# Weight splits shared out by turns, and zero products beside the weight statistics, in an attention-and-MLP kernel

## The chip, the core and the metric

The kernel runs on one core of a Trainium2 chip. The metric is device time in microseconds (us), the median of the runs. TensorE (PE in the profile, with its weight loads as PEld) multiplies, VectorE (DVE), ScalarE (ACT) and GpSimd (POOL) work element by element, and SyncE (SP) and ScalarE issue the DMAs. Each engine works through its own queue in order.

## What is computed

Causal attention with a linear memory read beside it, and a gated MLP behind it:

```python
scores = scale * q @ k.T                       # B, H, S, D = 4, 8, 576, 64, causal
local = softmax(scores) @ v
q_p = where(q > 0, q, exp(q) - 1) + 1
mem_out = (q_p @ M_prev) / (q_p @ z_prev + 1e-6)
attn = g * mem_out + (1 - g) * local           # g = sigmoid(beta), per head
x = attn.reshape(2304, 512)
xn = x / sqrt(mean(x * x) + 1e-6) * rms_g
h = silu(xn @ w_gate) * (xn @ w_val)           # 512 -> 1536
out = h @ w_out                                # 1536 -> 512
```

The weights arrive as 64-bit floats. Products are made exact enough by splitting each operand into a 16-bit high part and a 16-bit low part and adding three products (high with high, high with low, low with high).

## The kernel before, in words

The 2304 tokens are 18 blocks of 128 rows; two blocks form a chunk of 256, so there are nine chunks. Attention runs block by block in units of one to four heads: scores (line 443, PE), scaling and mask (L449, DVE), exponential (L495, ACT), high part (L497, ACT), low part (L506, DVE, or POOL for blocks 2 and 3), transposition (by PE for blocks 0 and 1, by DMA from block 2 on) and the product with v (L530 to L532). A finished block is normed and split into x (`x_split`, L621). A chunk's projections need x of both of its blocks.

**The weights.** `w_gate` and `w_val` are cut into 24 pieces of 128 x 512: three thirds t of the 1536 columns, in each eight pieces p. A piece passes four steps. `load_w` (L659) brings its raw words into a ring of five places; the load of piece p+5 is issued from ACT's queue once piece p is converted. `w_conv` (L975) converts it: ACT L687 and DVE L691 and L692 write one float32 piece into the tile `wgv`. `gram` (L128, products on L135) forms sums of squares on PE, from which `gv_scales` (L702) makes the third's scales `rgs` once its eighth piece is through. `w_split` (L737) then scales the piece and splits it into high and low part. With `SPLIT` at "3" (`split`, L89) this is: DVE scales in place (L99), ACT rounds to the high part (L101), POOL subtracts for the low part (L104). `w_out` passes the same steps in twelve pieces of its own (`wo_conv`, `wo_split`, tile `wo`).

**Places in `wgv`.** The tile has 25 places, and a place holds either one float32 piece or one pair of high and low part. Piece p lies as float32 in place p+1 and its split goes into place p. So a split writes where the piece before it was read from: the high part of piece p+1 (L101) waits until POOL has finished L104 of piece p. At the start, places 17 to 24 hold the early k and v blocks that `first_gram` reads.

**Projections.** For column block F of a chunk, `m_proj` (L750) makes 24 products of 128 x 256 into `gv` (L762), `m_act` (L765) and `m_split` (L778) form the hidden values, and `m_down` (L805, L816 to L818) multiplies them with `w_out`. The names gv0 to gv11 below are chunk 0's column blocks; gv0 to gv3 need the first third of the weights, gv4 to gv7 the second, gv8 to gv11 the last. gv12 begins chunk 1.

**What sets the order.** The program is written as lists of steps that are dealt out beside each other (`zipped`, `run`, L1049 to L1077): conversion and splitting of third 0 beside the first two blocks, of third t beside the projections of the third before it. The framework's scheduler then fixes the order in each engine's queue from priorities and its own idea of durations, so that a change of one step moves others.

Of the kernel before, what the change touches and what calls it, by code (L numbers as in the profile page):

```python
# [9 lines left out]
F32 = mybir.dt.float32  # L10
F16 = mybir.dt.float16
BF16 = mybir.dt.bfloat16
# [19 lines left out]
A3 = 0.2  # L32
A4 = 0.3
C2 = 8
SPLIT = ("3", "3", "3", "3")
VWAY = "11"
RING = 5
PACE = 5
NTP = 2
PRIO = (500, 600, 100)  # L40
NPM = 2
NPOOL = (4, 8)
# [3 lines left out]
def attn_memory_moe_kernel(  # L46
# [81 lines left out]
    def gram(acc, src, first, last):  # L128

        hi = src.bitcast(BF16).rearrange("p (f w) -> p f w", w=2)[:, :, 1]
        for g in range(4):
            w = hi[:, g * P : (g + 1) * P]
            nc.tensor.matmul(acc[:, :P], w, w, start=first and g == 0, stop=last and g == 3)  # L135

    csum = {}

# [97 lines left out]

    def load_pre(n):

        at = 1 + 4 * NC + 2 * (n - NI)
        pre[n] = wgv[:, at : at + 2, :]  # L240
        nc.sync.dma_start(out=pre[n], in_=qkv[n, :, :2, :])

# [390 lines left out]
    def piece(m, cc, t):  # L633
        return t * 2 * NC + m * NC + cc

    raws = {}
    NR = RING

# [63 lines left out]
    def gv_scales(t):  # L702
# [1 line left out]

        c = wt[:, t]
        mx = tiny.tile([P, 2], F32, tag="mx", name="wmx", bufs=2)
        nc.vector.tensor_reduce(mx, csum.pop(t), axis=AX.X, op=ALU.max)
        nc.vector.tensor_scalar(c[:, 6:8], over_partitions(mx, 2), gmax2, 1.03, op0=ALU.mult, op1=ALU.mult)
        pow2_scales(c[:, 6:8], 2, c[:, 0:2], c[:, 2:4])

# [25 lines left out]

    def w_split(m, cc, t):  # L737
        p = piece(m, cc, t)
        src = wgv[:, p + 1, :]
        sc = rgs[:, t, m, cc : cc + 1]  # L740
        split(wgv16[:, p, :512], wgv16[:, p, 512:], src, sc, way_of(SPLIT, t, p % (2 * NC)))

# [232 lines left out]
    def w_conv(i):  # L975
        m, cc, t = pcs[i]
        p = piece(m, cc, t)
        f64_to_f32(raws.pop(p), wgv[:, 1 + p, :], i)
        held.pop(p)
        if cc == m == 0:  # L980
            csum[t] = ps.tile([P, 2, P], F32, tag="out", name="csum")
        gram(csum[t][:, m], wgv[:, 1 + p, :], cc == m == 0, cc == NC - 1 and m == 1)
        if i + PACE < len(pcs):
            load_w(*pcs[i + PACE])

    def wo_conv(f):
        f64_to_f32(raws.pop(("o", f)), wo[:, 1 + f, :], len(pcs) + f)
        held.pop(("o", f), None)
        if f == 0:
            csum["o"] = ps.tile([P, 512], F32, tag="out", name="csum")  # L990
        gram(csum["o"], wo[:, 1 + f, :], f == 0, f == NF - 1)
        for nx in {0: (3,), 1: (4,), 2: (5,), 3: (6,), 4: (7,), 6: (8, 9), 8: (10,), 10: (11,)}.get(f, ()):
            load_wo(nx)

# [144 lines left out]
```

## Time and profile before

| what | us |
|---|---|
| median of three runs (lowest, highest) | 685.72 (685.72, 687.58) |
| the profiled execution's own time | 687.62 |
| its span, first to last instruction | 685.9 |
| PE busy in the span (2592 products of L762 alone) | 597.1 (363.4) |
| DVE, ACT, POOL busy | 480.8, 406.9, 232.3 |
| mean granted TensorE clock, as a share of 2.4 GHz | 0.938 |

A slice of the page is 685.9 / 40 = 17.1 us. Busy digits are tenths of a slice; the PEclk line gives the clock granted to TensorE in tenths of 2.4 GHz, so that 5 stands for 1.2 GHz all through and what lies between for a mixture. Shares over the whole span hide that the first 184 us and the rest have different limits, so the stretches are read apart.

### The profile page before, as it was taken

The page shows a single profiled execution, that of the slowest core. Times are in us where ns is not written, and L with a number is a line of the kernel's source. Part 1 is how long each engine was busy: PE and PEld are TensorE (multiplying, and loading weights), DVE is VectorE, ACT ScalarE, POOL GpSimd, SP SyncE. Part 2 cuts the span into 40 slices and gives each one's busy share as a digit, 9 for nine tenths or more (in the row PEclk, how much of TensorE's full clock was granted, in tenths as well). Part 3 has the DMA queues.
Part 4 walks back from the last instruction along what each step waited for, and adds up shares of the span by engine and source line. Part 5 has one row for each costly group of instructions (what it writes and reads, how often), then busy time and mean ns, then how long its engine had stood idle before and what let it go on. Part 6 is the DMA issues. An engine that isn't in the chain of part 4 may idle for free.

```text
span 685.9 us, 16422 instructions
## 1 busy us (share of the span) xinstructions
PE 597.1 (87%) x6292; PEld 461.3 (67%) x6292; DVE 480.8 (70%) x1441; ACT 406.9 (59%) x845; POOL 232.3 (34%) x308
## 2 busy tenths in 40 slices
PE   2664367866899999999899999999999999999997
PEld 1553245745665587778678777767777878887774
DVE  3689997985685766679687776786887686873221
ACT  5788655665647676657556657766666464442322
POOL 1306544674467434323025231431322222212111
PEclk9985567977899999999999999999999999999999
DMA  8952589833935968844675865376664554441001
GB/s 271 411 148 83 188 272 227 184 77 80 176 69 89 191 126 166 166 88 88 118 155 123 167 131 113 64 137 142 123 131 103 107 78 93 80 76 34 32 1 31
DMA packets 186383, 88.13 MB, mean 128 GB/s; under 512 B 171712, under 2 KB 171712, under 8 KB 186304
## 3 DMA queue, kind: packets, MB, share of 16 engines
q1 hardware_dynamic: 181392, 70.81, 49.5%
q10 hardware_dynamic: 4912, 16.28, 7.1%
q8 instruction: 49, 0.80, 0.5%
q14 instruction: 30, 0.25, 0.1%
HBM read 36.20 MB, written 4.72 MB: 60 GB/s over the span
## 4 chain that ended last, share of the span: by engine, by line
PE 43%; DVE 17%; DMA 16%; ACT 13%; issue 5%; POOL 4%; SPq 1%; ACTq 0%; DVEq 0%; POOLq 0%
PE gv L762 23%; DMA kv<-in_qkv_dram 6%; DMA PT<-P 5%; PE out L816 4%; PE out L817 4%; PE out L818 4%; DVE S L449 3%; ACT junk L220 2%; PE sc L443 2%; DMA qT<-row 2%; ACT P L497 2%; PE sc L469 2%; ACT S L495 2%; DVE P L506 2%; DMA phT<-row 2%
## 5 line engine op out<-in xcount | busy, mean ns | idle before, releaser
L762 PE MATMUL gv<-xT,wgv 128*128 128x256 f16 x2592 | 363.4, 279 | 11.7 <-DVE th L772 6.4
L762 PEld LDWEIGHTS <-wgv 128*128 128x128 f16 x2592 | 253.2, 100 | 56.0 <-issue 7.6
L794 POOL TENSOR_TENSOR h<-th,h 128x256 f16<-128x256 f32 x96 | 71.5, 745 | 259.3 <-ACT h L793 201.2
L495 ACT ACTIVATE S<-S,nm 128x128 f32<-128x128 f32 (+4 forms) x144 | 80.2, 586 | 57.3 <-DVE nm L456 42.2
L443 PE MATMUL sc<-kT,qT 128*128 128x128 f16 x640 | 94.9, 224 | 12.9 <-DMA kT<-row 4.1
L506 DVE TENSOR_TENSOR P<-S,P 128x512 f16<-128x512 f32 (+2 forms) x80 | 61.0, 763 | 40.4 <-ACT P L497 39.7
L769 DVE SCALAR_TENSOR_TENSOR th<-th,gv 128x256 f32<-128x256 f32 x108 | 44.9, 416 | 61.0 <-ACT th L768 60.6
L768 ACT ACTIVATE th<-gv,wt 128x256 f32<-128x256 f32 x108 | 50.4, 467 | 59.4 <-PE gv L762 56.2
L449 DVE CUSTOM_DVE_ANT_0 S<-sc,mask,qsc 128x128 f32<-128x128 f32 (+3 forms) x128 | 66.6, 545 | 12.6 <-PE sc L443 12.0
L817 PE MATMUL out<-wo,h 128*128 128x512 f16 x192 | 72.8, 379 | 0.0
L816 PE MATMUL out<-wo,h 128*128 128x512 f16 x192 | 72.6, 379 | 0.1
L818 PE MATMUL out<-wo,h 128*128 128x512 f16 x192 | 71.8, 379 | 0.0
L443 PEld LDWEIGHTS <-qT 128*128 128x128 f16 x640 | 56.6, 100 | 21.9 <-issue 8.0
L497 ACT CAST P<-S 128x512 f16<-128x512 f32 (+2 forms) x104 | 62.2, 599 | 10.2 <-DMA PT<-P 9.0
L793 ACT CAST h<-th 128x256 f16<-128x256 f32 x96 | 38.5, 402 | 44.7 <-DVE th L772 44.2
L530 PE MATMUL loc<-v,PT 128*128 128x65 f16 x320 | 55.4, 197 | 5.7 <-DMA PT<-P 5.3
L532 PE MATMUL loc<-v,PT 128*128 128x65 f16 x320 | 54.9, 197 | 2.0 <-ACT PT L347 2.0
L531 PE MATMUL loc<-v,PT 128*128 128x64 f16 x320 | 54.9, 197 | 0.0
L772 DVE SCALAR_TENSOR_TENSOR th<-th,wt,gv 128x256 f32<-128x256 f32 x108 | 51.6, 478 | 1.9
L605 POOL TENSOR_TENSOR t<-t,t 128x256 f32<-128x256 f32 x36 | 31.4, 873 | 60.0 <-DVE t L601 57.7
L530 PEld LDWEIGHTS <-PT 128*128 128x128 f16 x320 | 31.6, 100 | 14.2 <-DMA PT<-P 10.8
L104 POOL TENSOR_TENSOR wgv<-wgv 128x512 f16<-128x512 f32 x24 | 31.7, 1321 | 26.8 <-ACT wgv L101 26.6
(222 smaller groups left out, 1104.4 us busy)
## 6 DMA issues: line engine op xcount, KB each, us to landing
kv<-in_qkv_dram SPq DMA_DIRECT2D x18, 512.0 KB, 4.8
wo<-in_moe_w_val_dram ACTq DMA_DIRECT2D x11, 512.0 KB, 4.7
q<-in_qkv_dram SPq DMA_DIRECT2D x18, 256.0 KB, 3.5
wo<-in_moe_w_gate_dram ACTq DMA_DIRECT2D x8, 512.0 KB, 6.0
wo<-in_moe_w_out_dram ACTq DMA_DIRECT2D x8, 512.0 KB, 5.1
qT<-qT SPq DMA_DIRECT2D x32, 128.0 KB, 2.6
out_dram<-res SPq DMA_DIRECT2D x16, 256.0 KB, 2.3
wo<-in_moe_w_gate_dram SPq DMA_DIRECT2D x4, 512.0 KB, 6.5
```

Source lines behind the costliest of these rows:

```text
L443: nc.tensor.matmul(t[:, g * w + j * P : g * w + (j + 1) * P], qT[n][:, t2, h, :], kT[blk_of[(b, j)]][:, h, :], start=(t2 == 0), stop=(t2 = ...
L449: nc.vector.tensor_tensor_reduce(out=s[:, g * w : (g + 1) * w], in0=t[:, g * w : (g + 1) * w], in1=mask[:, m0 : m0 + w], scale=qsc[n][:, 5:6],
L495: nc.scalar.activation(v_, v_, AF.Exp, bias=nm[:, g : g + 1], scale=-1.0)
L497: nc.scalar.copy(p16[:, : G * w], s[:, : G * w])
L506: eng.tensor_tensor(p16[:, w : 2 * w], s[:, :w], p16[:, :w], ALU.subtract)
L530: nc.tensor.matmul(a, phi_, vhi, start=(j == 0), stop=False)
L531: nc.tensor.matmul(a[:, :D], phi_, vlo, start=False, stop=False)
L762: nc.tensor.matmul(o, lhs, xT[c][:, rhs, :], start=(cnt == 0), stop=(cnt == 3 * NC - 1))
L794: nc.gpsimd.tensor_tensor(h16[:, 1], th, h16[:, 0], ALU.subtract)
L816: nc.tensor.matmul(o, hh, whi, start=(f == 0), stop=False)
L817: nc.tensor.matmul(o, hh, wlo, start=False, stop=False)
L818: nc.tensor.matmul(o, hl, whi, start=False, stop=(f == NF - 1))
```

## The change

It has three parts. The places: the float32 pieces of every third now lie in places 17 to 24 (`words_at`), and the early k and v blocks move to places 9 to 16. The splits: `SPLIT` becomes "01", so that pieces take turns. Even ones go by way 0: ACT scales and rounds in one instruction (`hi_cast`, L82 before), DVE subtracts with the scale folded in (`lo_cast`, L85). Odd ones go by way 1: ACT scales in place (L97), ACT rounds (L101), POOL subtracts (L104). The zero products: after each piece's `gram`, except a third's last and `w_out`'s last, `keep_up` issues five products of a zero block of `mask` with 256 columns of the piece, added into columns of the statistics' bank that are not read.

```diff
-SPLIT = ("3", "3", "3", "3")
+SPLIT = ("01", "01", "01", "01")
+KEEP = 5
+    def keep_up(acc, src):
+
+        hi = src.bitcast(BF16).rearrange("p (f w) -> p f w", w=2)[:, :, 1]
+        for g in range(KEEP):
+            nc.tensor.matmul(acc, mask[:, :P], hi[:, : 2 * P], start=False, stop=False)
...
-        at = 1 + 4 * NC + 2 * (n - NI)
+        at = 1 + 2 * NC + 2 * (n - NI)
...
+    def words_at(p):
+
+        return 1 + 4 * NC + p % (2 * NC)
...
-        nc.vector.tensor_reduce(mx, csum.pop(t), axis=AX.X, op=ALU.max)
+        nc.vector.tensor_reduce(mx, csum.pop(t)[:, :2], axis=AX.X, op=ALU.max)
...
-        src = wgv[:, p + 1, :]
+        src = wgv[:, words_at(p), :]
...
-        f64_to_f32(raws.pop(p), wgv[:, 1 + p, :], i)
+        f64_to_f32(raws.pop(p), wgv[:, words_at(p), :], i)
         held.pop(p)
         if cc == m == 0:
-            csum[t] = ps.tile([P, 2, P], F32, tag="out", name="csum")
-        gram(csum[t][:, m], wgv[:, 1 + p, :], cc == m == 0, cc == NC - 1 and m == 1)
+            csum[t] = ps.tile([P, 4, P], F32, tag="out", name="csum")
+        last = cc == NC - 1 and m == 1
+        gram(csum[t][:, m], wgv[:, words_at(p), :], cc == m == 0, last)
+        if not last:
+            keep_up(csum[t][:, 2:4], wgv[:, words_at(p), :])
...
+        if f < NF - 1:
+            keep_up(csum["o"][:, 2 * P :], wo[:, 1 + f, :])
```

ACT's queue where third 0 is split and third 1's conversion begins (about 55 us). `x` is block 0's x, `kv` the v parts of later blocks, `wgv<-wo` a conversion. Before:

```order
L220 ACTIVATE junk,xs<-t_0_580 128x512
L82 ACTIVATE x_713<-t_0_580,xs 128x512
L101 CAST wgv<-wgv 128x512
L97 ACTIVATE kv_117<-kv_117,cb_92 128x512
...
L97 ACTIVATE kv_501<-kv_501,cb_92 128x512
L687 ACTIVATE wgv<-wo 128x512 x5
L347 CAST xT_716<-tp 128x4x128
L97 ACTIVATE kv_125<-kv_125,tcb_902 128x512
```

The same place now, where line numbers are higher by one to eleven (L83 is L82 of before, L98 is L97, L102 is L101, L698 is L687):

```order
L83 ACTIVATE wgv<-wgv,rgs 128x512
L98 ACTIVATE wgv<-wgv,rgs 128x512
...
L83 ACTIVATE x_746<-t_0_615,xs 128x512
L98 ACTIVATE kv_117<-kv_117,cb_92 128x512
...
L98 ACTIVATE kv_536<-kv_536,cb_92 128x512
L102 CAST wgv<-wgv 128x512
L98 ACTIVATE kv_125<-kv_125,tcb_943 128x512
L102 CAST wgv<-wgv 128x512 x3
L698 ACTIVATE wgv<-wo 128x512 x3
```

The first two rows stand there four times in turn: all eight pieces of third 0 begin ahead of x, the four odd pieces are rounded behind the `kv` rows, and only then come the conversions of third 1.

POOL's queue where the last third is split (about 135 to 162 us; `P` are low parts of attention units of blocks 2 and 3, `t` a block's sum of memory and local part, `h16v` hidden values, `xs` a block's norm). Before:

```order
L104 TENSOR_TENSOR wgv<-wgv 128x512 x2
L794 TENSOR_TENSOR h16v<-th,h16v 128x256
L104 TENSOR_TENSOR wgv<-wgv 128x512
L605 TENSOR_TENSOR t_2_1253<-t_2_1253,t_2_1533 128x256
L506 TENSOR_TENSOR P_1642<-S,P_1642 128x512
...
L506 TENSOR_TENSOR P_1838<-S,P_1838 128x512
L605 TENSOR_TENSOR t_3_1720<-t_3_1720,t_3_1902 128x256
L104 TENSOR_TENSOR wgv<-wgv 128x512 x2
L605 TENSOR_TENSOR t_3_1720<-t_3_1720,t_3_1902 128x256
L104 TENSOR_TENSOR wgv<-wgv 128x512
```

Now (L105 is L104 of before, L612 is L605, L513 is L506, L805 is L794):

```order
L105 TENSOR_TENSOR wgv<-wgv 128x512
L513 TENSOR_TENSOR P_1678<-S,P_1678 128x512
L612 TENSOR_TENSOR t_2_1320<-t_2_1320,t_2_1628 128x256
L805 TENSOR_TENSOR h16v<-th,h16v 128x256
L513 TENSOR_TENSOR P_1735<-S,P_1735 128x512
...
L105 TENSOR_TENSOR wgv<-wgv 128x512
L612 TENSOR_TENSOR t_3_1823<-t_3_1823,t_3_2020 128x256
L513 TENSOR_TENSOR P_1951<-S,P_1951 128x512
L105 TENSOR_TENSOR wgv<-wgv 128x512
```

Four weight subtractions stand among the attention's instead of eight, and none is left behind the last of them ahead of block 3's second `t`. On PE, the seven remaining statistics of third 2 with their zero products moved from ahead of gv2 and gv3 to behind gv3 and directly ahead of gv4; the scales' products of third 2 still stand behind gv5.

## Rows read from the trace of the kernel before

**Rows 1.** The page, part 2: TensorE's busy tenths and granted clock, 40 slices.

```profile
PE   2664367866899999999899999999999999999997
PEclk9985567977899999999999999999999999999999
```

**Rows 2.** Busy us (instructions) by stretch, then clock, DMA share, GB/s.

```profile
40.00:84.00 44.00, 21.14 (x204) 15.60 (x205) 38.55 (x137) 35.40 (x73) 20.28 (x22) 0.58 0.39 131
84.00:120.00 36.00, 24.70 (x196) 18.97 (x193) 31.77 (x65) 19.87 (x37) 16.30 (x13) 0.71 0.95 249
120.00:161.00 41.00, 30.15 (x316) 23.25 (x313) 32.55 (x97) 24.15 (x51) 28.78 (x27) 0.79 0.57 122
161.00:184.00 23.00, 17.17 (x132) 13.00 (x132) 15.66 (x45) 14.13 (x33) 8.07 (x13) 0.78 0.67 130
184.00:240.00 56.00, 52.14 (x503) 34.59 (x502) 40.22 (x125) 35.66 (x76) 35.38 (x39) 1.00 0.65 123
```

**Rows 3.** Timeline of PE (start, duration, work, count, wait before it).

```profile
85.08 7.01 PE L762 MATMUL gv<-xT,wgv 128*128 128x256 f16 x47
...
109.67 1.06 PE L567 MATMUL mem<-M,phT 128*128 128x65 f16 x16 [3.15 <-DMA phT<-row]
...
117.02 1.14 PE L762 MATMUL gv<-xT,wgv 128*128 128x256 f16 x9
...
121.37 2.78 PE L762 MATMUL gv<-xT,wgv 128*128 128x256 f16 x24
...
158.09 2.10 PE L762 MATMUL gv<-xT,wgv 128*128 128x256 f16 x10
...
179.11 5.02 PE L762 MATMUL gv<-xT,wgv 128*128 128x256 f16 x24 [0.26 <-DVE th L772]
```

**Rows 4.** Timeline of ACT around third 0's splits and third 1's conversion.

```profile
56.62 0.61 ACT L101 CAST wgv<-wgv 128x512 f16<-128x512 f32 x1
57.12 2.56 ACT L97 ACTIVATE kv<-kv,cb 128x512 f32<-128x512 f32 x4
59.59 2.88 ACT L687 ACTIVATE wgv<-wo 128x512 f32<-128x512 f32 x5
```

**Rows 5.** Timeline of POOL: last subtraction of thirds 0, 1 and 2.

```profile
89.61 1.49 POOL L104 TENSOR_TENSOR wgv<-wgv 128x512 f16<-128x512 f32 x1 [3.37 <-ACT wgv L101]
...
116.25 1.21 POOL L104 TENSOR_TENSOR wgv<-wgv 128x512 f16<-128x512 f32 x1
...
159.92 1.15 POOL L104 TENSOR_TENSOR wgv<-wgv 128x512 f16<-128x512 f32 x1
```

**Rows 6.** Groups by line and form: count, busy us, mean ns, idle before.

```profile
L99 DVE TENSOR_SCALAR wgv<-wgv,rgs 128x512 f32<-128x512 f32 x24 | 14.1, 640 | 0.0
L99 DVE TENSOR_SCALAR wo<-wo,wos 128x512 f32<-128x512 f32 x12 | 7.6, 703 | 0.0
L104 POOL TENSOR_TENSOR wgv<-wgv 128x512 f16<-128x512 f32 x24 | 31.7, 1321 | 26.8 <-ACT wgv L101 26.6
L104 POOL TENSOR_TENSOR wo<-wo 128x512 f16<-128x512 f32 x12 | 15.2, 1270 | 4.9 <-ACT wo L101 4.8
L85 DVE SCALAR_TENSOR_TENSOR x<-t,xs,x 128x512 f16<-128x512 f32 x18 | 13.9, 770 | 2.4 <-ACT x L82 2.1
```

**Rows 7.** Chain of waits, 130 to 165 us: shares by line, block 3's x.

```profile
by line: issue 18.4%; DVE wgv L99 13.0%; POOL wgv L104 8.9%; POOL t L605 7.5%; DVE wo L692 7.2%; DVE S L449 7.0%; POOL P L506 4.5%; DVE th L772 4.0%; DVE th L769 3.7%; DVE nm L456 3.4%; ACT junk L220 2.1%; DVE ph L397 2.0%; DVE rgs L714 2.0
...
164.29 0.65 DVE x L85
```

**Rows 8.** Timeline of all engines at 77 us: a DVE instruction beside POOL's.

```profile
77.44 1.41 POOL L104 TENSOR_TENSOR wgv<-wgv 128x512 f16<-128x512 f32 x1 [0.17 <-ACT wgv L101]
...
77.81 1.05 DVE L716 TENSOR_TENSOR wt<-wt 128x1 f32<-128x1 f32 x1
...
78.99 0.14 DVE L717 TENSOR_SCALAR wt<-wt 128x1 f32<-128x1 f32 x1
```

**Rows 9.** Chain of waits, whole span: the transfer ahead of block 3.

```profile
98.77 10.86 DMA phT<-row
```

## The prediction

> **What bounds the kernel now.** The slices come first [rows 1]: from the twelfth on PE is at 9 tenths or more in nearly every slice, at the full 2.4 GHz; before that it is at 2 to 8 tenths and the clock lies between 1.2 and 2.4 GHz. The stretches say the same in microseconds [rows 2]: from 184 to 240 us PE is busy 52.14 of 56, while from 84 to 184 it is busy 24.70 + 30.15 + 17.17 = 72.0 of 100. So the end is a full queue of products behind a front that does not feed it. A microsecond saved anywhere behind 184 us on another engine is worth little; a microsecond by which the front reaches gv12 sooner is worth a microsecond. gv12, which begins chunk 1, starts at 179.11 [rows 3] and needs block 3's x, which DVE finishes at 164.29 + 0.65 [rows 7].
>
> What the front waits for is read in three places. gv0 and gv1 run from 85.08 to 92.1 [rows 3] and end a microsecond behind the last subtraction of third 0, at 89.61 + 1.49 = 91.1 [rows 5]. gv4 starts at 117.02 [rows 3] as the last subtraction of third 1 is under way, 116.25 to 117.46 [rows 5]. Third 2 ends at 161.1 [rows 5], and in the chain of waits from 130 to 165 us the scaling on DVE holds 13.0% of 35 us = 4.6 us and the subtraction on POOL 8.9% = 3.1 us [rows 7]. In all three the eight pieces of a third follow one another, since a piece's high part may be written only when POOL is through with the piece before it. Beside them stands a transfer, the transposition of block 2's phi(q), 10.86 us from 98.77 on [rows 9], which the products of block 2's memory wait for until 109.67 [rows 3].
>
> **The change part by part.** *Places.* Thirds 0 and 1 lose the chain from piece to piece; third 2 keeps it, as its float32 places 17 to 24 and its targets 16 to 23 still overlap by one. In exchange a piece of third 1 can be converted only when the piece of third 0 in its place is split, and likewise third 2 behind third 1. ACT now begins all eight splits ahead of block 0's x: 8 x 0.64 us (four instructions of that kind take 2.56 [rows 4]) = 5.1 us, and rounds the odd four ahead of the first conversion (3 more than before, about 0.5 us apart = 1.5 us). The first conversion, at 59.59 [rows 4], comes 6.6 us later. DVE's reduction of third 1's statistics stands ahead of block 1's x in its queue, so some of that reaches gv0; against it stand the splits of third 0, done by about 70 instead of 91.1 us. I take gv0 3 us later, 88, and gv1's end about where it is. Third 1's scales come some 4 us later, at 88; 5.1 us of first acts, four roundings between conversions and four subtractions of 1.3 us [rows 6] end by about 103 instead of 117.5. What is late next for gv4 is PE's own queue, where seven statistics of third 2 now stand ahead of it, with loads that start later. I take gv4 from 117 to 114: **-3 us**, bounds +4 (the delay of gv0 is kept) and -8 (half of 117.5 - 103 is kept; the shorter wait for the transposition counts in this, as weight loads no longer crowd it).
>
> *Splits, DVE.* The 24 + 12 scalings go, 14.1 + 7.6 = 21.7 us; 18 subtractions come. `wgv` shows none of that form, so the nearest row is x's low part, 0.770 us [rows 6]: 18 x 0.770 = 13.9. DVE is relieved by 7.8 us in all. *POOL.* 18 of 36 subtractions go, half of 31.7 + 15.2 = 23.5 us. *ACT.* 18 more instructions, 18 x 0.64 = 11.5 us; it is busy 19.87 of 36 us and 24.15 of 41 [rows 2], so I put this at nothing but for the 5.1 us at 55 us, which the item above has. If that cover failed, third 2's 4 x 0.64 = 2.6 us would count. On the path is what lies between 120 and 161 us: 4.6 us of DVE scaling and half of POOL's 3.1, together 6.1; four new DVE subtractions, 3.1 us, come in, but in a stretch where DVE is busy 32.55 of 41. Bounds -8 and -1; I take **-5 us**, nearer to the 6.1, since the scalings stood in one row in the chain and the new ones stand apart. Behind 184 us the same for `w_out` is worth at most the 3.9 us in which PE is idle until 240 us; I take **-1**.
>
> One behaviour can turn the DVE item round. At 77.81 an instruction on one column takes 1.05 us where its like takes 0.14, and it ends as POOL's subtraction does, 77.44 + 1.41 [rows 8]. The Trainium skill, SBUF — State Buffer, section Who interferes with whom, says that a DVE instruction with two SBUF inputs and a GpSimd instruction that reads SBUF exclude each other, and the later one waits. The 18 new DVE subtractions have two such inputs. By that rule each could be held like the row at 77.81, and DVE's account would stand at 18 x 0.9 - 7.8 = 8 us worse instead of 7.8 better. No more is drawn from it here: the 18 x subtractions of before are of that form too, and their mean of 0.770 [rows 6] already holds what they met, beside twice as many POOL subtractions.
>
> *Zero products.* (24 - 3) + (12 - 1) = 32 pieces x 5 = 160 products of 128 x 256. The trace has none of them; the nearest rows are the projections of the same size: 2.78 / 24 = 0.116 us at the full clock and 2.10 / 10 = 0.21 at half [rows 3]. All of them are 18.6 to 33.6 us of PE, and those behind 84 us (7 pieces of third 2, 11 of `w_out`: 90) 10.4 to 19. PE is idle 28.0 us between 84 and 184 [rows 2], and what is hidden is hidden there; if it were not, the whole 10.4 would count. They stand ahead of gv4 and among attention's products. I take **+2 us**, bounds 0 and +10. They should also keep PE's clock up: at a mean granted clock of 0.71, 0.79 and 0.78 [rows 2] the time at half rate is 58, 42 and 44%, so about 14.3 + 12.7 + 7.6 = 34.6 us of PE's work ran at half rate, and 17 us would be saved if none did. Most of this is PE waiting less long for the same inputs; I take **-1**, bounds 0 and -9 (half).
>
> Sum: -3 - 5 - 1 + 2 - 1 = -8 us. The profiled execution took 687.62, so 679.6; it stands 1.9 us above the median of 685.72, and on that the forecast is **678 us** (677.7).
>
> **The rivals.** *Slower: PE's and ACT's queues in the front.* The conversions of third 1 start 6.6 us later, and all that stands behind them in ACT's and DVE's queues, block 1's x among it, goes with them; then the zero products ahead of gv4 find no idle time. It decides if gv0 starts later than about 92, where third 0's splits ended before: +4 from the first item at its bad end, +10 for the zero products, -5 for the splits, -1 for `w_out`: +8, 694 us. For it speaks the order of ACT's queue, against it the 28 idle us and the 14 us by which third 1's splits end sooner.
>
> *No change.* What sets block 3's x is the attention of blocks 2 and 3 with its transpositions, one of 10.86 us [rows 9], and the relieved engines wait there instead: 685 us. For it speaks that "issue" has the largest share of that chain [rows 7]; against it that two of its four largest shares are the scaling and subtraction of weights.
>
> *Much faster: the clock stays up.* The first item at -3, the splits at -6, `w_out` -1 and the clock at its end of -9, with +2 for the products: -17, 669 us. The clock fell where PE was busy 21.14 of 44 us and 24.70 of 36, and is full from 184 on with 52.14 of 56 [rows 2]. The Trainium skill, TensorE: Matmul & The Clock Gate, section What's actually happening, says that activity releases the throttle and idling brings it back; by it the zero products fill just such gaps, and this rival's 669 is what comes of it. The trace agrees as to the fall, and shows nothing on whether these products are enough.
>
> *It does not do what it says:* the products run and the granted clock stays as it is. That takes 1 us from the forecast and is within it.
>
> **How the numbers follow.** Forecast, 672 to 683 us: 0.46. Much faster, 664 to 672: 0.16. No change, 683 to 688: 0.18. Slower, 688 to 698: 0.20. About 0.3% (2 us) is what a measurement of this kernel tells from no change: below 683.7 is faster, above 687.8 slower. That gives faster 0.62, same 0.18, slower 0.20. Leaving out a tenth at either end, the range is 667 to 692.
>
> **What would show it.** Right: L99 gone from DVE, 18 L104 instead of 36, third 1's last weight subtraction near 103 us, gv4 near 114, block 3's x near 157, gv12 near 171, and PE busy from there on as before. The second item is right if third 2's last split ends before 157. The clock item is right if the granted clock between 84 and 184 us rises above 0.9 while the zero products take about 0.12 us each. Wrong: gv0 later than 92, or products that stand ready while PE works off zero products; then the places cost more than the chain did.

## The result, and the profile after

The changed kernel took 692.9 us, the median of four runs (692.66 to 693.01), against 686.65 for the kernel before in the same number of runs: a ratio of 1.009, 95% interval 1.007 to 1.011. It is 6 us slower; the forecast was 678, in a range of 667 to 692, so the sign was wrong and the time lies just outside the range. The profiled execution took 692.66 with a span of 690.9. Ratios are formed from the undisturbed runs, so they can differ a little from the quotient of two medians.

The page of the changed kernel, part 2, answers to [rows 1]: TensorE's busy tenths and granted clock in 40 slices of 17.3 us.

```profile
PE   2872677786799898999899999999999999999997
PEclk9976679998999999999999999999999999999999
```

The clock line is higher than before in the front: its fourth to eleventh digits were 55679778 and are 66799989. The stretches (columns as in [rows 2]) say it in numbers, and the last row is the page's group of the zero products of the weights:

```profile
84.00:120.00 36.00, 27.14 (x237) 21.55 (x238) 27.16 (x82) 22.80 (x44) 7.76 (x6) 0.86 0.75 168
120.00:161.00 41.00, 32.05 (x365) 26.36 (x364) 35.58 (x102) 29.33 (x60) 22.80 (x23) 0.92 0.80 195
161.00:184.00 23.00, 15.42 (x122) 12.05 (x122) 14.43 (x34) 12.05 (x27) 9.06 (x15) 0.87 0.27 61
184.00:240.00 56.00, 50.96 (x509) 34.68 (x507) 40.08 (x125) 41.64 (x86) 23.90 (x29) 0.99 0.71 136
...
L142 PE MATMUL csum<-wgv,mask 128*128 128x256 bf16 x105 | 20.2, 334 | 0.0
```

The clock rose from 0.71, 0.79 and 0.78 to 0.86, 0.92 and 0.87, and POOL is relieved. Yet the kernel is slower, so a higher clock and a lighter POOL do not by themselves shorten it. The timelines show where it loses. First those of ACT, POOL and DVE (start, duration, work, wait), in the order of the front:

```profile
67.39 1.76 ACT L698 ACTIVATE wgv<-wo 128x512 f32<-128x512 f32 x3
...
94.74 0.66 ACT L698 ACTIVATE wgv<-wo 128x512 f32<-128x512 f32 x1
...
106.96 0.39 ACTq L687 DMA_DIRECT2D wo<-in_moe_w_out_dram  x1
...
160.48 1.15 POOL L105 TENSOR_TENSOR wgv<-wgv 128x512 f16<-128x512 f32 x1 [2.48 <-ACT wgv L102]
...
169.38 0.75 DVE L86 SCALAR_TENSOR_TENSOR x<-t,xs,x 128x512 f16<-128x512 f32 x1
```

The marks of the kernel before that stand in no row above (ACT, PE and DVE; `rawo` is the raw form of a late piece of `w_out`, `loc` the product of attention with v, `row` a split row of block 4's q):

```profile
79.41 2.32 ACT L687 ACTIVATE wgv<-wo 128x512 f32<-128x512 f32 x4
...
85.31 0.33 ACTq L676 DMA_DIRECT2D wo<-in_moe_w_out_dram  x1
...
148.04 0.67 ACT L687 ACTIVATE wo<-rawo 128x512 f32<-128x512 f32 x1
...
158.04 0.25 PE L532 MATMUL loc<-v,PT 128*128 128x65 f16 x1
...
161.13 0.39 PE L762 MATMUL gv<-xT,wgv 128*128 128x256 f16 x2 [0.93 <-POOL wgv L104]
...
166.79 0.75 DVE L85 SCALAR_TENSOR_TENSOR row<-q,qsc,row 128x512 f16<-128x512 f32 x1
```

Third 1's first conversion comes at 67.39 (59.59 before, [rows 4]); third 2's first at 94.74, where before it came at 79.41; the first load of `w_out` at 106.96 instead of 85.31; third 2's last split at 160.48, as late as before ([rows 5]: 159.92); and block 3's x ends at 169.38 + 0.75 = 170.1 instead of 164.9 [rows 7]. Block 3's x is 5.2 us later, and the profiled execution is 692.66 - 687.62 = 5.0 us longer.

What the front now waits for is shown by the chain of waits of the whole span, where it passes here (start, duration, work; `th` are steps of the hidden values):

```profile
145.93 3.92 DMA rawo<-in_moe_w_out_dram
...
153.15 4.13 DMA rawo<-in_moe_w_out_dram
157.30 1.00 DVE rawo L702
...
159.09 0.67 DVE wgv L86
...
159.78 0.63 ACT wgv L102
...
160.48 1.16 POOL wgv L105
...
161.69 0.30 PE gv L773
...
163.78 7.08 PE gv L773 x48
...
171.39 0.42 DVE th L780
...
175.61 1.91 DVE row L86 x2
```

`load_wo` puts pieces 6, 8, 10 and 11 of `w_out` through one buffer (`bufs=1`), so each load waits for the conversion of the one before it. DVE stands until 157.30 before the last of them; queued behind it are third 2's last subtraction (159.09), ACT's rounding, POOL's last subtraction, and the products of chunk 0 that need it (161.69). In the kernel before the same last conversion ran at 148.04, ahead of all this.

From there on two things are late. The chain goes through gv10 and gv11 (163.78) to DVE, where the scales of block 4's q stand behind gv11's hidden values (171.39), so that block 4's first row starts at 175.61 (166.79 before). Beside the chain, block 3's x is late because the last part of its attention now stands on PE behind the products that wait for the last split. In the kernel before it stood ahead of them (158.04 and 161.13 above); now:

```profile
161.69 0.39 PE L773 MATMUL gv<-xT,wgv 128*128 128x256 f16 x2 [0.62 <-POOL wgv L105]
161.91 0.19 PE L537 MATMUL loc<-v,PT 128*128 128x65 f16 x1
```

### The profile page after: what moved, and what is told of

Its sections match the earlier page's. It is cut to its first block, busy times and chain, and to the rows that moved or that the text cites. A ratio compares the mean times of both kernels' runs of the same rounds, so it can differ in the third digit from the quotient of the medians.

```text
span 690.9 us, 16723 instructions
## 1 busy us (share of the span) xinstructions
PE 608.6 (88%) x6452; PEld 473.0 (68%) x6452; DVE 469.9 (68%) x1423; ACT 417.3 (60%) x863; POOL 205.2 (30%) x290
## 4 chain that ended last, share of the span: by engine, by line
PE 51%; DMA 20%; ACT 11%; DVE 10%; issue 4%; POOL 2%; SPq 1%; ACTq 0%; POOLq 0%; DVEq 0%
PE gv L773 27%; DMA PT<-P 7%; PE out L828 4%; PE out L827 4%; PE out L829 4%; PE sc L450 3%; DMA kv<-in_qkv_dram 3%; DMA wo<-in_moe_w_val_dram 3%; DMA qT<-row 2%; DMA xT<-x 2%; PE sc L476 2%; DMA kT<-row 1%; ACT junk L227 1%; ACT row L83 1%; DVE S L456 1%
## 5 line engine op out<-in xcount | busy, mean ns | idle before, releaser
L773 PE MATMUL gv<-xT,wgv 128*128 128x256 f16 x2592 | 359.2, 277 | 12.4 <-DVE th L783 8.0
L805 POOL TENSOR_TENSOR h<-th,h 128x256 f16<-128x256 f32 x96 | 71.8, 748 | 274.9 <-ACT h L804 221.4
L450 PE MATMUL sc<-kT,qT 128*128 128x128 f16 x640 | 93.1, 223 | 7.2 <-DMA kT<-row 2.3
L513 DVE TENSOR_TENSOR P<-S,P 128x512 f16<-128x512 f32 (+2 forms) x80 | 60.4, 755 | 39.6 <-ACT P L504 39.0
L612 POOL TENSOR_TENSOR t<-t,t 128x256 f32<-128x256 f32 x36 | 28.6, 794 | 62.7 <-DVE t L608 60.3
L513 POOL TENSOR_TENSOR P<-S,P 128x512 f16<-128x512 f32 (+1 forms) x24 | 26.7, 1112 | 32.2 <-ACT P L504 26.3
```

Source lines behind the costliest of these rows:

```text
L450: nc.tensor.matmul(t[:, g * w + j * P : g * w + (j + 1) * P], qT[n][:, t2, h, :], kT[blk_of[(b, j)]][:, h, :], start=(t2 == 0), stop=(t2 = ...
L513: eng.tensor_tensor(p16[:, w : 2 * w], s[:, :w], p16[:, :w], ALU.subtract)
L773: nc.tensor.matmul(o, lhs, xT[c][:, rhs, :], start=(cnt == 0), stop=(cnt == 3 * NC - 1))
L805: nc.gpsimd.tensor_tensor(h16[:, 1], th, h16[:, 0], ALU.subtract)
```

## The experiments

An edit to this program moves more than itself, because the framework's scheduler lays every queue out anew. So the three parts of the change were run in all eight combinations, and then single links of the chain were undone. In each diff the minus side is the changed kernel unless another is named. The zero products are no part of the output; everything else is computed in full in every run. In the expectations theory W says that the late pieces of `w_out` cost the time, and theory O that the order of products in PE's queue behind 184 us does; theory Z blames the zero products, and in the runs that bind an order it stands for no difference. Each landmark is read from one profiled execution of a kernel, and executions of one kernel lie up to some 10 us apart, so a difference of a few us between the landmarks of two kernels can be chance.

**The parts one by one.** Without the zero products:

```diff
-KEEP = 5
+KEEP = 0
```

> The changed kernel without the zero products (KEEP = 0); places and splits stay as changed. Theory O (order): the loss against the kernel before arises behind 225 us, where PE waits for the transposed P of block 5's attention, because gv15 to gv19 (five times 24 products) now stand ahead of block 5's scores in PE's queue instead of between its parts. Here PE's queue is the same as in the changed kernel from block 4's scores on, so this run should lose the same 4 us behind 225 us: 688 to 692 us, and the granted clock between 84 and 161 us should fall back towards 0.7 to 0.8. Theory Z (zero products on the path): the 160 products are what costs, so this run should be at or below the kernel before: 679 to 686 us.

697.6 us, 1.0169 (1.0128 to 1.0210): slower still. Theory Z falls, and theory O's 688 to 692 is missed too. The clock fell back as expected (0.74 and 0.79 from 84 to 161 us). On the changed kernel the zero products give about 5 us.

The kernel before with the zero products alone (from the changed kernel: `SPLIT` back to "3", `words_at(p)` back to p + 1, `load_pre` back to 1 + 4 * NC):

> The kernel before with the zero products alone: places and splits of before. Theory Z: 5 to 8 us slower than before, 691 to 695 us. Theory O: PE's queue moves too, but about half as far (gv18 and gv19 are used up two units of block 5 earlier than before instead of five), so 687 to 690 us. The clock item of the prediction: granted clock between 84 and 161 us above 0.85 instead of 0.71 to 0.79.

694.0 us, 1.0100 (1.0067 to 1.0132), theory Z's value. Here the same products cost 7 us, although the clock rises as expected (0.87 and 0.92 in the stretches from 84 to 161 us). The price of one part depends on the others.

The places alone (`SPLIT` back to "3", `KEEP = 0`):

> The changed kernel with the splits of before (way 3) and no zero products: the places alone. The prediction's first item: -3 us, 683.5 us, with the last split of third 1 at about 103 to 108 us instead of 117.5. Theory O: PE's queue is moved as in the run with the zero products alone, which gives 2 us back: 685.5 to 688 us.

706.9 us, 1.0293 (1.0253 to 1.0332): 20 us slower, where the prediction's first item said 3 us faster. What the item promised at third 1 does come: its last split ends at 98.6 instead of 117.5, and gv4 starts at 115.1 instead of 117.0. But third 2's first conversion comes at 89.2 instead of 79.4, `w_out`'s first load at 104.1, and block 3's x ends at 181.6.

The splits in turn alone, on the kernel before:

```diff
-SPLIT = ("3", "3", "3", "3")
+SPLIT = ("01", "01", "01", "01")
```

> The kernel before with the splits in turn alone: places of before, no zero products. The prediction's second and third item: -5 and -1, 680.5 us, with third 2's last split before 157. Theory W: w_out's loads start as before (85 to 90), so block 3's x comes at 160 to 165: 680 to 686 us. Rival Q (queue): 48 more products are used up ahead of block 5's attention, as in the changed kernel, and 4 us are lost behind 225 us: 686 to 690 us.

1.0027 (0.9997 to 1.0058), twelve runs between 683.3 and 693.9 with a median of 691.3: no gain, neither the prediction's 680.5 nor W's 680 to 686. `w_out` starts early (88.06), but third 2's last split ends at 160.0 and block 3's x at 169.0 (in an execution of 692.35). By itself this says that theory W does not cover everything that can delay it.

Splits and zero products on the places of before:

```diff
-        at = 1 + 2 * NC + 2 * (n - NI)
+        at = 1 + 4 * NC + 2 * (n - NI)
...
-        return 1 + 4 * NC + p % (2 * NC)
+        return p + 1
```

> The changed kernel with the places of before: splits in turn and zero products. W: w_out's first load at 85 to 92 us, block 3's x at 163 to 167: 684 to 689 us, so that the places are what makes the change slower. Rival A (the edits add up): the splits alone took about 2 to 4 us and the zero products alone 7, so 694 to 698 us.

677.8 us, 0.9856 (0.9815 to 0.9896): the fastest of all, 15 us below the changed kernel and 9.7 below the kernel before beside it. Its timelines of ACT, PE, POOL and DVE, the same landmarks as above (the PE row is the sum over partitions that gives third 2's scales):

```profile
62.06 1.77 ACT L698 ACTIVATE wgv<-wo 128x512 f32<-128x512 f32 x3
...
80.05 2.86 ACT L698 ACTIVATE wgv<-wo 128x512 f32<-128x512 f32 x5
85.02 0.33 ACTq L687 DMA_DIRECT2D wo<-in_moe_w_out_dram  x1
...
110.92 0.38 PE L123 MATMUL allp<-ident,wmx 128*2 128x128 f32 x2
...
148.86 1.15 POOL L105 TENSOR_TENSOR wgv<-wgv 128x512 f16<-128x512 f32 x1 [2.27 <-ACT wgv L102]
...
156.75 0.75 DVE L86 SCALAR_TENSOR_TENSOR x<-t,xs,x 128x512 f16<-128x512 f32 x1
```

Against the changed kernel every landmark is earlier; the distance grows up to `w_out`'s first load and stays above 11 us behind it: 5.3 us at third 1's first conversion, 14.7 at third 2's, 21.9 at `w_out`'s first load, 13.9 at third 2's scales (124.77 in the changed kernel), 11.6 at third 2's last split, 12.6 at block 3's x.

Places and zero products without the splits (`SPLIT` back to "3"):

> The changed kernel with the splits of before (way 3): common places and zero products. The places alone took 706.9 us. By what the zero products gave on the changed kernel (697.6 to 692.9) and on the run with third 1's own places (691.8 to 686.8), 5 us less than that: 700 to 703 us. By what they cost on the kernel before (7 us more): 712 to 715 us. W: block 3's x stands behind w_out's last conversion and comes at 175 to 181.

697.1 us, 1.0141 (1.0104 to 1.0178): the zero products give 10 us here, more than expected. Block 3's x ends at 175.9, behind `w_out`'s last conversion (166.08), as W said. The eight together:

| places | splits | zero products | median, us | ratio to before | `w_out`'s first load | block 3's x ends |
|---|---|---|---|---|---|---|
| before | 3 | no | 685.7 to 687.4 | 1 | 85.3 | 164.9 |
| before | 01 | no | 691.3 | 1.0027 | 88.1 | 169.0 |
| before | 3 | yes | 694.0 | 1.0100 | 90.8 | 169.1 |
| before | 01 | yes | 677.8 | 0.9856 | 85.0 | 157.5 |
| new | 3 | no | 706.9 | 1.0293 | 104.1 | 181.6 |
| new | 01 | no | 697.6 | 1.0169 | 104.9 | 176.3 |
| new | 3 | yes | 697.1 | 1.0141 | 105.1 | 175.9 |
| new | 01 | yes | 692.9 | 1.009 | 107.0 | 170.1 |

By the medians the places cost 20, 6 and 15 us in three of the four pairs; the 3 us of the pair with the splits of before and zero products are not clear of noise (1.0141 against 1.0100, and the intervals overlap). `w_out`'s first load is 14 to 22 us later with them, and its last load stands on the chain of waits in all four, at 153 to 163 us; with the places of before no load through the single buffer stands there later than 139 us. The splits in turn give 16, 9 and 4 us in three pairs and nothing in the first.

**Which third.** Third 1's pieces back in place p + 1 (third 2's are the same by either rule, so only third 0 and the k and v blocks stay moved):

```diff
-        return 1 + 4 * NC + p % (2 * NC)
+        return p + 1 if 2 * NC <= p < 4 * NC else 1 + 4 * NC + p % (2 * NC)
```

> The changed kernel, but third 1's float32 pieces lie in place p+1 as before the change; thirds 0 and 2 keep places 17 to 24. So third 2's conversions wait for third 0's splits alone, and third 1 keeps the chain from piece to piece. Theory W: w_out's first load comes at 85 to 95 instead of 107, the last conversion of w_out before 152, block 3's x at 162 to 166: 683 to 688 us. Rival N: third 1's splits are later than in the changed kernel by up to 14 us, gv4 with them, and nothing is won: 692 to 696 us.

686.8 us, 1.0015 (0.9986 to 1.0045): W's value, 6 us better than the changed kernel, although third 1's last split now ends at 121.6 instead of 101.4. `w_out`'s first load is at 88.31, its last conversion at 145.18, block 3's x ends at 165.6. The other way round, third 0's pieces in their own places and third 1 moved (`p + 1 if p < 2 * NC`):

> The changed kernel, but third 0's float32 pieces lie in place p+1 as before; thirds 1 and 2 keep places 17 to 24. It is the counterpart of the run with third 1's own places (686.8), in which only third 0 is moved; with neither moved the time was 677.8, with both 692.9. If third 0's move costs by late conversions of third 1 (first conversion at 67.4 instead of 62.1 us) and third 1's move by late conversions of third 2 and late loads of w_out, the two add up and this run loses the 6 us of third 1's move alone: 682 to 686 us, with third 1's first conversion at 60 to 63 and w_out's first load behind 100 us. If w_out's late loads matter only beside third 0's move: 677 to 680 us.

690.8 us, 1.0063 (1.0032 to 1.0094). `w_out`'s first load is at 103.40, as expected, but the time is above both values: moving third 1 alone costs 13 us, third 0 alone 9, both 15. They do not add up. Both make block 3's x late (168.1 and 165.6, against 157.5 with neither).

Third 1's own places with the splits of before and no zero products:

> The run with the places alone (splits of before, no zero products), with third 1's float32 pieces in place p+1 as before the change. Theory W: of the 20 us that the places alone cost, nearly all go, since third 2 no longer waits for third 1: 685 to 690 us, block 3's x at 163 to 168 instead of 181.6. Rival F (front): it is third 0's shared places that cost, and 700 us or more stay.

698.6 us, 1.0165 (1.0137 to 1.0192): 8 of the 20 us go, not nearly all, so third 0's move costs too. And with the splits in turn, without zero products:

> The run with third 1's own places (686.8 us) without the zero products. Theory K: the products pay by the clock, as without them the changed kernel took 697.6 instead of 692.9: the granted clock between 84 and 161 us falls from about 0.87 to 0.75 and the time rises by 3 to 6 us, to 690 to 693 us. Rival M: the products only moved the order in the changed kernel, and cost PE time where PE is not idle: 681 to 686 us.

691.8 us, 1.0052 (1.0016 to 1.0087): 5 us slower than with them, theory K's value; what carries the gain is tested below.

**The link at 157 us.** In the changed kernel, an order alone is bound: `w_out`'s pieces 9 to 11 behind block 3's x on ACT and DVE.

```diff
+        if p >= 6 * NC + 9:
+            after(begun[p], xdone[3], "x first")
+            after(shift, xlow[3], "x first")
```

> The changed kernel; only the order of two queues is bound: the conversions of w_out's pieces 9, 10 and 11 (ACT's and DVE's first instruction of each) stand behind block 3's x. Theory W (w_out's pieces): with the common places third 2's conversions wait for third 1's splits, w_out's loads start 21.6 us later (106.96 instead of 85.31), and the last pieces, which pass one after the other through a single buffer with a load of about 4 us each, now stand in ACT's and DVE's queues ahead of third 2's last splits and of block 3's x: DVE and ACT wait until 157.30 for a load issued at 153.15. Block 3's x then comes at 170.1 instead of 164.9, and the end moves with it. By W block 3's x ends at 163 to 166 here and the time is 686 to 689 us. Rival N (the wait hides behind other work): x stays at 168 to 170 and the time at 691 to 694 us.

686.9 us, 0.9997 (0.9972 to 1.0021): the 6 us are back. DVE's timeline, and below the second "..." the row of block 4's q in the changed kernel:

```profile
156.97 0.75 DVE L86 SCALAR_TENSOR_TENSOR wgv<-wgv,rgs 128x512 f16<-128x512 f32 x1 [2.58 <-ACT wgv L83]
...
166.09 0.75 DVE L86 SCALAR_TENSOR_TENSOR x<-t,xs,x 128x512 f16<-128x512 f32 x1
167.22 0.42 DVE L702 TENSOR_SCALAR rawo<-rawo 128x512 int32<-128x512 int32 x1
168.77 0.75 DVE L86 SCALAR_TENSOR_TENSOR row<-q,qsc,row 128x512 f16<-128x512 f32 x1
...
175.61 1.24 DVE L86 SCALAR_TENSOR_TENSOR row<-q,qsc,row 128x512 f16<-128x512 f32 x1
```

The last subtraction of third 2 and block 3's x no longer wait for `w_out`, which is converted behind them without harm. Block 3's x comes only 3.3 us sooner (166.84; 163 to 166 was expected), but block 4's row, which the chain ran through, comes 6.8 us sooner, and the profiled executions differ by 692.66 - 685.87 = 6.8 us. The reverse test is the kernel before with late loads of `w_out`:

```diff
+        if f < 3:
+            after(ins, begun[23], "late")
```

> The kernel before, places and splits of before, no zero products; only the first three loads of w_out are bound behind the last conversion of third 2 in ACT's queue, so that they start at about 112 us instead of 85. Theory W (w_out's pieces): a late w_out alone is enough: its last conversion moves from 148 to 155 to 160 us, block 3's x from 164.9 to 168 to 172, and the time to 690 to 695 us. Rival V: w_out has slack in the kernel before, and what delays block 3's x in the changed kernel is the splits or the zero products themselves: block 3's x at 164 to 166, time 685 to 688 us.

683.3 us, 0.9935 (0.9905 to 0.9965), faster than before. The expectation's 112 us was a misreading: third 2's conversions run from 79.4 to 91.2 in the kernel before and from 79.0 to 89.7 here (those of the changed kernel end at 110.9), so the loads began at 89.77, only 4.5 us late. This is no test of W, and why the run is 4 us faster no run isolates; a binding can thus give some us by the new order alone, which holds for the 6 us of the run above too but for its landmarks. Bound to a rounding of third 1's split (`rounded[13]`) instead:

> The kernel before; only the first three loads of w_out are bound behind the rounding of third 1's sixth piece in ACT's queue, which comes at about 110 us, so that w_out's loads start about 25 us later while third 2's conversions stay where they are. In ACT's queue the last conversion of w_out then stands between block 2's x and block 3's x, as in the changed kernel. Theory W: that is enough, block 3's x comes at 168 to 173 instead of 164.9 and the time is 690 to 696 us. Rival V: late loads have slack, block 3's x at 163 to 166 and the time at 683 to 688 us; then the late loads cost only beside the splits of the changed kernel, whose last ones stand in DVE's and ACT's queues behind them.

687.4 us, 1.0004 (0.9979 to 1.0030). Now the loads begin at 107.18, as in the changed kernel, the last conversion runs at 156.49, and block 3's x ends at 169.7, as late as W said; yet nothing is lost. So W in its simple form falls: late loads are not enough, and block 3's x gives the time to some microseconds only. POOL's and PE's timelines of this run:

```profile
147.55 1.16 POOL L104 TENSOR_TENSOR wgv<-wgv 128x512 f16<-128x512 f32 x1
...
154.04 4.09 PE L765 MATMUL gv<-xT,wgv 128*128 128x256 f16 x36
```

What differs from the changed kernel is third 2's last subtraction, at 147.55 instead of 160.48, ahead of `w_out`'s last pieces and not behind them, so that gv10 and gv11 ran from 154.04 instead of 163.78 and were done when block 3's x came. That fits the run above; no run isolates it.

**The order behind 184 us.** In PE's queue the changed kernel has 29 to 48 more products of chunk 1 ahead of the parts of block 4's scores, and 36 down to 21 more ahead of those of block 5; PE then waits behind 220 us. Here gv15 to gv19 are bound behind parts of these scores:

```diff
+    PIN = {(15, 0): (4, 3), (16, 0): (4, 5), (17, 0): (4, 7), (18, 1): (5, 2), (19, 0): (5, 3)}
+                if cnt == 0 and (F, m) in PIN:
+                    after(ins, last_sc[PIN[(F, m)]], "order")
```

> The changed kernel with five dependencies that only bind the order in PE's queue: gv15 behind the fourth unit of block 4's scores, gv16 behind the sixth, gv17 behind the eighth, gv18's second half and gv19 behind the third and fourth unit of block 5's. So these products stand between the parts of block 5's attention about where they stood before the change. Nothing is computed otherwise. Theory O: the wait for the transposed P behind 225 us goes and with it about 4 us: 687 to 689.5 us. Theory Z: no change against the changed kernel, 692 to 694 us.

691.7 us, 1.0065 (1.0033 to 1.0097). The stretch from 220 to 290 us in the kernel before, the changed kernel and this run, in that order:

```profile
220.00:290.00 70.00, 67.19 (x745) 50.44 (x742) 48.77 (x141) 48.88 (x102) 28.95 (x38) 1.00 0.83 160
...
220.00:290.00 70.00, 62.48 (x677) 45.54 (x675) 47.35 (x136) 48.49 (x101) 30.35 (x39) 1.00 0.78 144
...
220.00:290.00 70.00, 67.76 (x726) 50.38 (x725) 46.28 (x135) 48.64 (x100) 26.80 (x36) 1.00 0.76 149
```

PE's 5 us there do come back, and the time hardly moves, since most of those products are then missing earlier (from 184 to 220 us PE is busy 31.23 us instead of 34.59). Theory O's value was 687 to 689.5, so the order holds 1 to 2 us of the 6 at most, which the interval can't tell from nothing. The late front is the loss; where PE shows it is a matter of order. The same binding on the runs with third 1's own places and with block 3's x first:

> The run with third 1's own places (686.8 us) and gv15 to gv19 bound behind parts of block 4's and 5's scores as in the pinned run. Theory O (order): the waits for the transposed P behind 215 us (4.6 us) go and 2 to 3 us are kept: 683 to 685 us. Rival Z (zero sum): what PE does not work off early it works off later, no difference beyond 1.5 us: 685.5 to 688 us.

> The run with block 3's x ahead of w_out's last conversions (686.9 us) and gv15 to gv19 bound as in the pinned run. Theory O: the waits for the transposed P behind 215 us (4.9 us) go, 2 to 3 us are kept: 683 to 685 us. Rival Z: no difference beyond 1.5 us: 685.5 to 688.5 us.

685.8 (0.9969, 0.9941 to 0.9997) and 684.9 (0.9966, 0.9931 to 1.0002): 1 to 2 us better by the medians, 2 to 3 by the ratios, at the edge of what can be told, between the two theories.

**What the zero products give.** Splits and zero products on the places of before, with 16 columns instead of 256:

```diff
-            nc.tensor.matmul(acc, mask[:, :P], hi[:, : 2 * P], start=False, stop=False)
+            nc.tensor.matmul(a2[:, :16], mask[:, :P], hi[:, :16], start=False, stop=False)
```

> The run with splits in turn and zero products on the places of before (677.8 us), with products of 16 columns instead of 256. Their number is the same and PE's order from block 4's scores on is the same, but they occupy PE for little time. If the zero products give their 13 us by keeping PE's clock up: the granted clock between 84 and 120 us falls from 0.94 to about 0.75 and the time rises to 686 to 691 us. If they give it by the order of the queues that the scheduler lays out around them: 676 to 681 us at the lower clock.

680.1 us, 0.9870 (0.9819 to 0.9922): of the 13.5 us between 691.3 and 677.8, 11 remain. The group of these products for the weights, and the stretches from 84 to 161 us, of this run; below the "..." the same stretches with 256 columns:

```profile
L144 PE MATMUL csum<-wgv,mask 128*128 128x16 bf16 x105 | 6.5, 179 | 0.0
84.00:120.00 36.00, 28.08 (x303) 23.33 (x303) 30.44 (x77) 24.90 (x47) 9.45 (x9) 0.88 1.01 251
120.00:161.00 41.00, 29.81 (x325) 22.91 (x323) 31.67 (x97) 27.49 (x59) 24.28 (x26) 0.71 0.58 121
...
84.00:120.00 36.00, 32.92 (x327) 27.90 (x324) 33.42 (x74) 26.15 (x49) 10.66 (x10) 0.94 1.02 282
120.00:161.00 41.00, 30.82 (x328) 24.09 (x329) 29.96 (x102) 27.84 (x60) 23.06 (x29) 0.83 0.47 100
```

With a third of the PE time most of the gain stays. In the first stretch the clock fell less than expected (0.88, not 0.75). Over both, from 84 to 161 us, it is 0.79, no higher than in the run with the splits alone (0.81, 691.3 us); with 256 columns it is 0.88. So most of the gain is not the clock's: it comes with the order that the scheduler lays out around 160 more instructions. Whether the last 2 us are the clock's can't be told.

**A version that adds the findings up.** Third 1's own places, the bound gv15 to gv19, and `w_out`'s loads behind third 2's last conversion:

> The run with third 1's own places and gv15 to gv19 bound (685.8 us), with w_out's first three loads bound behind third 2's last conversion as in the run that took 683.3, where this drew third 2's conversions ahead. If both gains add up: 681 to 683 us, faster than the kernel before by 0.6 to 0.9%. If they are the same gain, or the late loads push w_out's conversions into block 3's x: 685 to 688 us.

680.3 us, 0.9897 (0.9860 to 0.9934): better than both by the ratios (0.9935 and 0.9969), though its interval touches that of the first. The expectation repeats the misreading above: third 2's conversions were not drawn ahead (82.5 to 92.9 us here), and `w_out`'s first load moved from 87.5 to 93.6. Simply leaving the places as they were is at least as good (677.8; the intervals overlap).

## Why the prediction was wrong

**The step that failed is the first item, the places.** It was put at -3 us with bounds of +4 and -8, and measured +15 beside the other two parts, +6 and +20 in two other pairs, and +3, not clear of noise, in the fourth. Its working followed the new wait one third far: third 1's conversions behind third 0's splits, 6.6 us at ACT (7.8 measured), gv0 at 88 (87.4 measured), third 1's last split at 103 (101.4 measured), gv4 at 114 (116.09 measured). The shorter transposition that its bounds count on came too: 5.9 us from 97.34 instead of 10.86. It named the same wait for third 2 behind third 1, and then looked only at gv4 and put what stands behind third 2's conversions at nothing. But third 2's conversions moved with it, from 79.4 to 94.7, and since `w_out`'s loads stand behind them in ACT's queue and use raw places that they free, `w_out`'s first load moved from 85.3 to 107.0 and its last conversion from 148.0 to 157.3, ahead of third 2's last split. Of the 16 us by which third 1's splits ended sooner, 0.9 reached gv4 and nothing gv10 (163.74 before, 163.78 now); with third 1's own places they end 20 us later than in the changed kernel, and the time is 6 us shorter.

**The splits, -5 us and -1,** have no fixed value either: 4 us beside the other two parts, 9 and 16 in two other pairs, nothing alone. With zero products on the places of before, third 2's last split ran at 148.86 and block 3's x ended at 157.5, the landmarks that the prediction gave (before 157, near 157); alone, the splits reached neither (160.0 and 169.0). With the places the splits end at 161.6, behind the wait of DVE and ACT for `w_out` until 157.30; with that wait taken away (the run that binds block 3's x first) they still end at 159.6. The working by engine held: 12 subtractions of `wgv` on DVE took 802 ns on average (0.770 taken), DVE fell by 10.9 us in all (7.8 worked out), POOL by 27.1 (23.5), ACT rose by 10.4 (11.5). What did not hold is that such a saving is a gain on the path by itself: the splits alone gave nothing (1.0027).

**The rule of the Trainium skill on DVE and POOL** (SBUF — State Buffer, Who interferes with whom) was weighed and put aside, rightly as to most of these subtractions: by a hold of each, 0.9 us would have come on top of the 0.770, and the mean is 0.802. Ten of the 12 took 0.72 to 0.75 us; the two that ran beside POOL's work on `t` (59.81 to 60.64) and `P` (147.11 to 148.27) took 1.09 and 1.12. It is seen at more cost elsewhere (below).

**The zero products, +2 us and the clock, -1.** They took 20.2 + 8.8 = 29.0 us of PE (18.6 to 33.6 given), and the clock rose to 0.86, 0.92 and 0.87 (above 0.9 was asked for). As a sum on the path the item has no fixed value: +7 on the kernel before, -5 to -14 in the other three pairs, and in the one pair where it was tested mostly by order rather than by PE time or clock. The rival "much faster" put the clock at up to 9 us; with 16 columns and the clock from 84 to 161 us at 0.79 instead of 0.88 the time differs by 2.3 us, which the two intervals can't tell from nothing.

**Chunk 1's start was misread.** The prediction took the row at 179.11 in [rows 3] for gv12. PE's timeline of the kernel before has these rows ahead of it, and the changed kernel has the two below the "...":

```profile
163.74 6.37 PE L762 MATMUL gv<-xT,wgv 128*128 128x256 f16 x44 [2.22 <-DVE th L772]
...
170.53 3.22 PE L762 MATMUL gv<-xT,wgv 128*128 128x256 f16 x28
...
163.78 7.07 PE L773 MATMUL gv<-xT,wgv 128*128 128x256 f16 x48 [1.34 <-DVE th L783]
...
173.03 4.64 PE L773 MATMUL gv<-xT,wgv 128*128 128x256 f16 x41 [2.18 <-DVE qsc L118]
```

44 + 28 = 72 products are gv10, gv11 and gv12, so gv12 began near 171 and 179.11 is gv13. gv12 thus came 2 us later after the change, not 8 us earlier. The number stood in no term of the sum, but it made chunk 1's start look as if it stood apart from chunk 0's end. In the kernel before gv12 followed gv11 with PE idle for 0.29 us only; in the changed kernel PE is idle for 2.18 us ahead of it, and it starts 2.9 us behind block 3's x.

**The rivals.** "Slower" gave 694 us and had the right sign and size, but its mechanism is not what happened: gv0 was at 87.4, not behind 92, and the zero products do not cost beside the other two parts (without them it took 697.6). Its first half, that what stands behind third 1's conversions goes with them, was right one third later. "No change" said that the attention of blocks 2 and 3 with its transpositions sets block 3's x and the relieved engines wait there. In the changed kernel the last part of that attention itself waits on PE, behind the split that waited for `w_out`.

**What stays open.** Why third 0's move (with the k and v blocks) costs 9 us by itself, when its `w_out` is early, and why the splits alone give nothing while the splits with 160 small products give 11 us. In each case the scheduler's order differs in many places at once, and no run separates them. Over the 20 profiled kernels block 3's x ends between 157.5 and 181.6, and the time of the same execution lies 515 to 525 us behind it; so the end of the front is what these edits move, with up to 10 us that block 3's x does not tell.

## What to carry to other kernels

When buffers are shared between stages, follow the new wait through all the stages that use them, to the last load of the program, and not only to the next consumer; what is freed early at one place is paid where the next stage can't start. A queue that serves several streams in order makes a late load cost whatever was laid behind it, so look at what stands behind a wait before pricing it. And where a scheduler lays the queues out anew, the prices of single edits don't add up: here the three parts took +0.3, +1.0 and +2.9% alone, two of them together -1.4%, so such a change is worth running part by part.

## What the runs showed of the hardware

A DVE instruction with two inputs was held beside POOL's subtractions: DVE's and POOL's timelines of the changed kernel.

```profile
68.07 4.36 DVE L703 SCALAR_TENSOR_TENSOR wgv<-wgv,wo 128x512 int32<-128x512 int32 x3 [4.89 <-ACT wgv L698]
...
73.61 0.68 DVE L703 SCALAR_TENSOR_TENSOR wgv<-wgv,wo 128x512 int32<-128x512 int32 x1
...
65.39 4.97 POOL L105 TENSOR_TENSOR wgv<-wgv 128x512 f16<-128x512 f32 x4 [4.69 <-ACT wgv L102]
70.32 3.09 POOL L105 TENSOR_TENSOR v<-kv,v 128x512 f16<-128x512 f32 x2
```

Three took 4.36 us, 1.45 each, while POOL ran from 65.39 to 73.41, and the next one, behind POOL's end, 0.68. Each held one ended 0.55 to 0.56 us behind the end of a POOL instruction (69.34, 70.90 and 72.43 behind 68.78, 70.35 and 71.88). This is the rule that the prediction cited, on another instruction than the one it was weighed for: it held the conversions, of which the common places put three beside a row of POOL's splits. Over all 24 the mean is 853 ns, against 717 in the kernel before and 685 in the fastest run. It goes the other way too: in the kernel before, POOL's sum on `t` at 62.72 took 3.51 us beside five conversions of 0.68 to 0.69 us each, and 0.84 at 74.13 without one.

Unexpected was also how little a higher clock is worth where PE waits for others: with the zero products alone it went from 0.71 and 0.79 to 0.87 and 0.92 between 84 and 161 us, and the kernel took 694.0 us instead of 686.4.
